# Last block of an attention plus SwiGLU kernel: products P5 and P3 in two PSUM banks, P3 one token tile at a time, the first two token tiles stored in three pieces

## The chip, the cores and the metric

The kernel runs on one core of one Trainium2 chip. The metric is the device time of one execution in microseconds (us), so less is better. A profile of one execution is at hand: every instruction of every engine with its start and duration, and every DMA packet.

## The reference

Attention without a softmax, normalised per head, feeds a gated feed-forward block. Everything is float32.

```python
kv = np.einsum('bhsd,bhse->bhde', k, v)
out = np.einsum('bhsd,bhde->bhse', q, kv)
rms = np.sqrt(np.mean(out * out, axis=-1, keepdims=True) + 1e-06)
x = out / rms * g_norm          # (8, 8, 576, 64), brought to (4608, 512)
g = x @ w_gate                  # (512, 1536)
silu = g * (1.0 / (1.0 + np.exp(-g)))
val = x @ w_val                 # (512, 1536)
result = silu * val @ w_out     # (1536, 512) -> (4608, 512)
```

## The kernel before, in words

The 4608 tokens are cut into nine blocks of 512 (`BLK`), a block into four token tiles of 128. For each block the kernel makes x (attention, transposed), then the hidden values h (the "up" products with w_gate and w_val, silu and multiplication), then the output ("down", the product with w_out). Most large products are done in a Strassen-Winograd form: seven products P1 to P7 of half-size matrices stand in for eight, with sums and differences made by VectorE (DVE) and GpSimd (POOL). From block 2 on the up part applies the form twice, and its prepared weights are streamed from DRAM by the SP queue (line 655).

The class `Down` makes the output of a block. `Ffn.down` (line 835) runs its products in the order 1, 5, 6, 7, 2, 4, 3. `CHAIN` (line 401) says which of three PSUM accumulators a product goes to: 1, 6, 7 and 4 to "b", 2 to "a", 5 and then 3, on top of it, to "c". An accumulator is one PSUM tile of 128 partitions x 2 x 256 float32: two token tiles e = 0 and e = 1, each with 256 output columns. The pool of "c" has two buffers, "b" three, "a" one. `Quad.multiply` (line 420) issues the matmuls of one product: for each e and each of six steps i over the hidden dimension one 128x256 matmul, which the profile shows as two PE matmuls. `Down.order` (line 744) sorts them by i, so e = 0 and e = 1 take turns and both token tiles are complete only with the last matmul.

When a product is complete its `after` function takes the accumulator out:

- after P7 (line 770): ScalarE (ACT) copies "b", DVE adds "c" (P5 alone so far) to it and writes `o2[:, :, HD:DM]`, the right 256 columns of token tiles 2 and 3
- after P2 (line 764): DVE adds "a" and the saved P1 and writes `o1[:, :, 0:HD]`, the left columns of token tiles 0 and 1; then it makes one more difference of h, which P3 reads
- after P4 (line 777): ACT copies "b" to the left columns of `o2`, and `Ffn.store` (line 791) sends `o2` to the output
- after P3 (line 781): DVE adds "c" and the saved P6 (`u2`), writes the right columns of `o1`, and `store` sends `o1`

A store is one DMA on the SP queue, 128 partitions x 2 token tiles x 512 columns, which is listed as 512 KB. Each engine and the SP queue take their instructions in the order in which the program was written; a framework adds the semaphore waits, tile by tile. In the last block (n = 8) nothing follows: after P3 there are one DVE addition, one store and the end of the program.

Of the kernel before, what the change touches and what calls it, by code (L numbers as in the profile page):

```python
# [8 lines left out]
F32 = mybir.dt.float32  # L9
# [5 lines left out]
P = 128  # L15
# [3 lines left out]
def kernel(  # L19
# [41 lines left out]
    nc = tc.nc  # L61

    B, H, S, D = q.shape
    NT, DM = out.shape
    FF = moe_w_gate.shape[1]
    T = 4
    BLK = P * T
    HB = BLK // 2
    HD = DM // 2
    NB = NT // BLK  # L70
# [39 lines left out]
    add = lambda e, o, a, b: e.tensor_tensor(out=o, in0=a, in1=b, op=OP.add)  # L110
# [3 lines left out]
    def ring():  # L114

        return r_pool.tile([P, 4, BLK], F32, name="r")

    class Words:
# [12 lines left out]
        def __init__(self, src, shape):  # L131
            self.raw = ld_pool.tile([P, 2 * BLK], U32, name="ld")
            dst = self.raw.rearrange("p (a b) -> p a b", a=shape[0])
            nc.sync.dma_start(out=dst, in_=src)
            self.shape = shape
# [267 lines left out]
    PSUMS = {"a": a_psum, "b": b_psum, "c": c_psum}  # L403
# [6 lines left out]
    class Quad:  # L410


        def __init__(self, steps):
            self.steps = steps
            self.ps, self.room = {}, None

        def prepare(self):
            pass

        def multiply(self, p):  # L420
            name, first = CHAIN[p]
            if first:
                self.ps[name] = PSUMS[name].tile([P, 2, HB], F32, name=name)
            for e, i in self.order(p):
                lhsT, rhs = self.operands(p, e, i)

                nc.tensor.matmul(  # L427
                    self.ps[name][:, e], lhsT=lhsT, rhs=rhs, start=first and (e, i) == (0, 0),
                    stop=i == self.steps - 1, skip_group_check=True,
                )  # L430
            getattr(self, f"after{p}", lambda: None)()

        def order(self, p):
            return [(e, i) for e in range(2) for i in range(self.steps)]
# [14 lines left out]
    class Up(Quad):  # L449
# [22 lines left out]
        def after2(self):  # L472
            add(nc.vector, self.s, self.ps["a"], self.s)
            nc.scalar.activation(out=self.s, in_=self.s, func=ACT.Silu)

        def after7(self):
            self.u3 = self.piece(2)
            nc.scalar.copy(out=self.u3, in_=self.ps["b"])
            add(nc.vector, self.u3, self.ps["c"], self.u3)
# [6 lines left out]
        def after3(self):  # L486
            add(nc.vector, self.u2, self.ps["c"], self.u2)
            mul(nc.gpsimd, self.h[:, :, 0:HB], self.s, self.u2)
            self.ffn.ended = self.ffn.h_sums(self.j, 1, nc.vector)
# [225 lines left out]
    class Down(Quad):  # L715
        def __init__(self, ffn):
            super().__init__(NP)
            self.ffn = ffn
            self.t = {}

        def turn_t(self, p, after=None):

            pairs = wo.rearrange("p (j e) d -> p e j d", e=2)
            of = {5: pairs[:, 1, :, HD:DM], 7: pairs[:, 0, :, 0:HD], 4: pairs[:, 1, :, 0:HD]}[p]
            self.t[p] = []
            for i in range(0, NP, 2):
                t = t_tile((self.ffn.n, p))
                turned = sub(nc.gpsimd, t, of[:, i : i + 2], pairs[:, 0, i : i + 2, HD:DM])
                if after:
                    tc.add_manual_dep(  # L730
                        turned.ins, after.ins.name,
                        mybir.DependencyInfo(mybir.DependencyClass.Sync, mybir.DependencyReason.DATA), reason="order",
                    )
                self.t[p] += [t[:, 0], t[:, 1]]
# [8 lines left out]

        def order(self, p):
            order = [(e, i) for e in range(2) for i in range(self.steps)]
            return sorted(order, key=lambda ei: ei[1])

        def operands(self, p, e, i):
            h = self.ffn.h
# [13 lines left out]

        def after2(self):
            add(nc.vector, self.o1[:, :, 0:HD], self.ps["a"], self.s)

            pairs = self.ffn.h.rearrange("p (j e) t -> p e j t", e=2)
            sub(nc.vector, pairs[:, 1, :, 0:HB], pairs[:, 1, :, 0:HB], pairs[:, 0, :, HB:BLK])

        def after7(self):  # L770
            o = ring()
            self.o1, self.o2 = o[:, 0:2], o[:, 2:4]
            u3 = self.piece(2)
            nc.scalar.copy(out=u3, in_=self.ps["b"])
            add(nc.vector, self.o2[:, :, HD:DM], self.ps["c"], u3)

        def after4(self):
            nc.scalar.copy(out=self.o2[:, :, 0:HD], in_=self.ps["b"])
            self.ffn.store(self.o2, 2)

        def after3(self):
            add(nc.vector, self.o1[:, :, HD:DM], self.ps["c"], self.u2)
            self.ffn.store(self.o1, 0)

    class Ffn:
        def __init__(self, n, att):
# [1 line left out]
            self.h = h_pool.tile([P, NF, BLK], F32, name="h")  # L788
            self.ps, self.making, self.leaf_room, self.ended = {}, [], None, None

        def store(self, o, t):
            rows = out[BLK * self.n : BLK * (self.n + 1), :].rearrange("(t p) d -> p t d", t=T)
            nc.sync.dma_start(out=rows[:, t : t + 2, :], in_=o)

        def h_sums(self, j, k, engine):

# [105 lines left out]
    for n in range(NB):  # L902
        ffn = Ffn(n, blocks[n])
# [76 lines left out]
```

## Time and profile before

| | |
|---|---|
| time, median of 4 runs | 1067.55 us (1066.72 to 1067.89) |
| the profiled execution's own time | 1066.43 us |
| its span, first to last instruction | 1064.5 us |
| around the span | 1.93 us |
| PE matmul busy | 1039.0 us, 98% of the span |
| DVE, POOL, ACT busy | 66%, 34%, 23% of the span |
| last matmul of P3 ends | 1059.82 us |
| last DVE addition | 1059.85 us, 0.69 us long |
| last store issued on SP | 1060.57 us |

The span runs from the first to the last instruction of the core; what the device time has beyond it lies before or after. A matmul's end in the trace is modelled; the chain of waits counts a product up to where the next work could start. PE is TensorE, SPq the queue from which SP issues DMAs. The time of a DMA in the rows of DMA issues runs from its issue to the landing of its last byte.

### The profile page before, as it was taken

What the parts mean: (1) busy time and instruction counts of PE and PEld (TensorE: products, weight loads), DVE (VectorE), ACT (ScalarE), POOL (GpSimd) and SP (SyncE); (2) the same over time, 40 slices, a digit from 0 to 9 for tenths busy, and PEclk for the clock granted to TensorE, in tenths of its full rate; (3) what the DMA queues carried; (4) which work ended last, traced back from release to release, by engine and by line L of the source; (5) the groups of instructions that cost most, each with busy time, mean ns of one, the idle gap of its engine ahead of it and who ended that gap; (6) DMA issues with size and microseconds to landing.
All of it is one profiled execution on the core that took longest, in us unless ns stands there. A gap on an engine that the chain in (4) does not pass through costs nothing.

```text
span 1064.5 us, 21799 instructions
## 1 busy us (share of the span) xinstructions
PE 1039.0 (98%) x8780; PEld 937.2 (88%) x8780; DVE 701.1 (66%) x1243; ACT 244.9 (23%) x392; POOL 365.5 (34%) x280
## 2 busy tenths in 40 slices
PE   5899999998999999999999999999999999999998
PEld 4644788877899989998999899989999899989997
DVE  2999596768656765676656666666667566755661
ACT  2665111211211211222112212121112211212110
POOL 0000453343025701472156305630455036602670
PEclk9899999999999999999999999999999999999999
DMA  9797103565578326742576247724782366126611
GB/s 242 223 267 226 57 20 101 158 175 162 172 207 243 103 78 190 236 141 61 173 237 174 77 134 231 213 56 131 226 226 70 97 197 192 47 80 203 188 31 40
DMA packets 154356, 161.87 MB, mean 152 GB/s; under 512 B 48400, under 2 KB 105104, under 8 KB 154256
## 3 DMA queue, kind: packets, MB, share of 16 engines
q1 hardware_dynamic: 154192, 160.48, 51.2%
q8 instruction: 70, 1.15, 0.4%
q14 instruction: 30, 0.25, 0.1%
q0 software_dynamic: 64, 0.00, 0.0%
HBM read 138.02 MB, written 22.41 MB: 151 GB/s over the span
## 4 chain that ended last, share of the span: by engine, by line
PE 90%; DVE 4%; SPq 2%; DMA 2%; POOL 1%; issue 1%; ACT 0%; POOLq 0%; DVEq 0%
PE b L576 25%; PE b L427 18%; PE c L576 12%; PE c L427 9%; PE a L576 6%; PE a L427 5%; PE b L861 4%; PE c L861 4%; PE m L339 2%; PE m L255 1%; PE m L292 1%; SPq L223 1%; DVE r L111 1%; DVE xi L111 1%; DVE r L110 1%; PE b L292 1%
## 5 line engine op out<-in xcount | busy, mean ns | idle before, releaser
L110 POOL TENSOR_TENSOR r<-r 128x256 f32<-128x256 f32 (+1 forms) x105 | 110.1, 1054 | 362.9 <-DVE r L110 357.6
L110 DVE TENSOR_TENSOR r<-b,r 128x512 f32<-128x512 f32 (+1 forms) x273 | 162.3, 607 | 61.3 <-PE b L576 56.5
L110 DVE TENSOR_TENSOR r<-c,r 128x512 f32<-128x512 f32 (+1 forms) x177 | 109.0, 626 | 99.3 <-PE c L576 56.0
L111 POOL TENSOR_TENSOR t<-wo 128x512 f32<-128x512 f32 x81 | 112.6, 1415 | 163.9 <-DVE wo L110 107.9
L576 PE MATMUL b<-x,t 128*128 128x128 f32 x1092 | 151.3, 276 | 0.0
L576 PEld LDWEIGHTS b<-x,t 128*128 128x128 f32 x1092 | 136.0, 192 | 0.6
L110 DVE TENSOR_TENSOR r<-a,r 128x512 f32<-128x512 f32 (+1 forms) x99 | 62.6, 633 | 83.2 <-PE a L576 53.1
L112 POOL TENSOR_TENSOR h<-r 128x1024 f32<-128x1024 f32 (+1 forms) x40 | 81.4, 2049 | 93.0 <-DVE r L110 79.7
L576 PE MATMUL c<-xi,t 128*128 128x128 f32 x840 | 112.1, 275 | 0.0
L576 PEld LDWEIGHTS c<-xi,t 128*128 128x128 f32 x840 | 102.8, 192 | 0.0
L427 PE MATMUL b<-t,h 128*128 128x256 f32 x432 | 97.1, 382 | 0.0
L427 PE MATMUL b<-wo,h 128*128 128x256 f32 x432 | 96.2, 379 | 0.0
L427 PEld LDWEIGHTS b<-wo,h 128*128 128x128 f32 x432 | 81.5, 190 | 10.6
L427 PEld LDWEIGHTS b<-t,h 128*128 128x128 f32 x432 | 80.8, 190 | 10.9 <-issue 0.2
L590 ACT COPY r<-b 128x512 f32<-128x512 f32 x63 | 36.9, 585 | 219.1 <-PE b L576 191.8
L576 PE MATMUL b<-xi,t 128*128 128x128 f32 x588 | 79.8, 276 | 0.0
L576 PEld LDWEIGHTS b<-xi,t 128*128 128x128 f32 x588 | 72.4, 192 | 0.0
L576 PE MATMUL b<-x,wg 128*128 128x128 f32 x336 | 53.0, 280 | 0.0
L576 PE MATMUL b<-x,wv 128*128 128x128 f32 x336 | 51.3, 275 | 0.0
L427 PE MATMUL c<-t,s 128*128 128x256 f32 x216 | 48.9, 383 | 0.0
L427 PE MATMUL a<-wo,h 128*128 128x256 f32 x216 | 48.3, 379 | 0.0
L427 PE MATMUL c<-wo,h 128*128 128x256 f32 x216 | 48.1, 379 | 0.0
(129 smaller groups left out, 1650.6 us busy)
## 6 DMA issues: line engine op xcount, KB each, us to landing
t<-w SPq DMA_DIRECT2D x336, 256.0 KB, 3.0
out_dram<-r SPq DMA_DIRECT2D x18, 512.0 KB, 2.9
ld<-in_q_dram SPq DMA_DIRECT2D x29, 256.0 KB, 4.5
ld<-in_moe_w_gate_dram SPq DMA_DIRECT2D x12, 512.0 KB, 5.3
ld<-in_moe_w_val_dram SPq DMA_DIRECT2D x12, 512.0 KB, 5.1
ld<-in_moe_w_out_dram SPq DMA_DIRECT2D x12, 512.0 KB, 4.4
w<-t SPq DMA_DIRECT2D x36, 128.0 KB, 2.1
ld<-in_k_dram SPq DMA_DIRECT2D x26, 160.0 KB, 3.4
```

The source lines that it names most:

```text
L110: add = lambda e, o, a, b: e.tensor_tensor(out=o, in0=a, in1=b, op=OP.add)
L111: sub = lambda e, o, a, b: e.tensor_tensor(out=o, in0=a, in1=b, op=OP.subtract)
L112: mul = lambda e, o, a, b: e.tensor_tensor(out=o, in0=a, in1=b, op=OP.mult)
L223: nc.sync.dma_start(out=t[r * D : (r + 1) * D, :, 0 : m * D], in_=src[self.n, hs, s0 : s0 + m * D].rearrange("h (p t) d -> p h (t d)", t=m),)
L255: nc.tensor.matmul(self.kv_ps[r][u * D : (u + 1) * D, j, :], lhsT=self.k[j][rows, u, c, :], rhs=self.v[j][rows, u, c, :], start=(c == 0), ...
L292: nc.tensor.matmul(self.ps[i][u][p : p + D, t, j, :], lhsT=self.qt[rows, 2 * i + t, j, p : p + D], rhs=kvs[b % 3][rows, j, :], start=True, ...
L339: nc.tensor.transpose(ps[:, e, t], xt[:, t, j + e], ident)
L427: nc.tensor.matmul(self.ps[name][:, e], lhsT=lhsT, rhs=rhs, start=first and (e, i) == (0, 0), stop=i == self.steps - 1, skip_group_check=True,
L576: nc.tensor.matmul(ps[:, i, f], lhsT=self.weight(o, p, f), rhs=self.operand(o, p), start=first and (i, f) == (0, 0), stop=True, skip_group ...
L590: nc.scalar.copy(out=dst, in_=ps)
L861: nc.tensor.matmul(t, lhsT=w[f // 2][:, i, P * (f % 2) : P * (f % 2 + 1)], rhs=x[:, i, of], start=(i == 0), stop=(i == NS - 1),)
```

## The change

Only the last block is touched. There, P5 and P3 get two "c" tiles, one per token tile, instead of one (`apart`); each of the two has its own bank, and only half of each is used. P3 runs all six steps for e = 0 and then all six for e = 1; P5 keeps the alternating order. Both DVE additions that read "c" are split in two, one per token tile (`add_c`). The left columns of `o1` are stored right after P2, and the right columns one token tile at a time after P3, so that `o1` goes out in three DMAs; `o2` is stored as before, now between the first and the second of them.

```diff
@@ class Quad @@
+            self.apart = {}
+
         def multiply(self, p):
             name, first = CHAIN[p]
             if first:
-                self.ps[name] = PSUMS[name].tile([P, 2, HB], F32, name=name)
+                tiles = [PSUMS[name].tile([P, 2, HB], F32, name=name) for _ in range(1 + (name in self.apart))]
+                self.ps[name], self.apart[name] = tiles[0], tiles[-1]
+            banks = self.ps[name], self.apart[name]
             for e, i in self.order(p):
                 lhsT, rhs = self.operands(p, e, i)
 
                 nc.tensor.matmul(
-                    self.ps[name][:, e], lhsT=lhsT, rhs=rhs, start=first and (e, i) == (0, 0),
+                    banks[e][:, e], lhsT=lhsT, rhs=rhs, start=first and i == 0 and (e == 0 or banks[0] is not banks[1]),
                     stop=i == self.steps - 1, skip_group_check=True,
                 )
@@ class Down @@
+            self.final = ffn.n == NB - 1
+            if self.final:
+                self.apart["c"] = None
...
         def order(self, p):
             order = [(e, i) for e in range(2) for i in range(self.steps)]
-            return sorted(order, key=lambda ei: ei[1])
+            return order if p == 3 and self.final else sorted(order, key=lambda ei: ei[1])
...
         def after2(self):
             add(nc.vector, self.o1[:, :, 0:HD], self.ps["a"], self.s)
+            if self.final:
+                self.ffn.store(self.o1[:, :, 0:HD], 0, slice(0, HD))
...
-            add(nc.vector, self.o2[:, :, HD:DM], self.ps["c"], u3)
+            self.add_c(self.o2[:, :, HD:DM], u3)
...
         def after3(self):
-            add(nc.vector, self.o1[:, :, HD:DM], self.ps["c"], self.u2)
-            self.ffn.store(self.o1, 0)
+            self.add_c(self.o1[:, :, HD:DM], self.u2)
+            if not self.final:
+                self.ffn.store(self.o1, 0)
+                return
+            for e in range(2):
+                self.ffn.store(self.o1[:, e : e + 1, HD:DM], e, slice(HD, DM))
+
+        def add_c(self, o, u):
+
+            if not self.final:
+                add(nc.vector, o, self.ps["c"], u)
+                return
+            for e, c in enumerate((self.ps["c"], self.apart["c"])):
+                add(nc.vector, o[:, e], c[:, e], u[:, e])
@@ class Ffn @@
-        def store(self, o, t):
-            rows = out[BLK * self.n : BLK * (self.n + 1), :].rearrange("(t p) d -> p t d", t=T)
-            nc.sync.dma_start(out=rows[:, t : t + 2, :], in_=o)
+        def store(self, o, t, columns=slice(None)):
+            rows = out[BLK * self.n : BLK * (self.n + 1), columns].rearrange("(t p) d -> p t d", t=T)
+            nc.sync.dma_start(out=rows[:, t : t + o.shape[1], :], in_=o)
```

## The prediction

> **What bounds the kernel now.** I read the page first, then the chain of waits of the last 35 us, then the timeline there, then the rows that price the pieces. The page:
>
> ```profile
> span 1064.5 us, 21799 instructions
> ...
> PE 1039.0 (98%) x8780; PEld 937.2 (88%) x8780; DVE 701.1 (66%) x1243; ACT 244.9 (23%) x392; POOL 365.5 (34%) x280
> ...
> PE 90%; DVE 4%; SPq 2%; DMA 2%; POOL 1%; issue 1%; ACT 0%; POOLq 0%; DVEq 0%
> ```
>
> TensorE is the bound, at 98% of the span and 90% of the chain that ended last. The change leaves the number of matmuls as it is, so it can only win where TensorE is already done. The instruction orders of the two programs, which carry no times, are the same on every engine up to P5 of the last block. So everything is decided after about 1028 us. The end of the chain of waits, in order of time (start, length, what):
>
> ```profile
> 1049.45 5.18 PE b L427 x24
> 1054.63 5.19 PE c L427 x24
> 1059.82 0.02 issue
> 1059.85 0.69 DVE r L110
> ```
>
> P4 and P3 run without a gap, 24 PE matmuls in 5.18 and 5.19 us, 0.216 us each. P3 ends at 1059.82, and until the span's end at 1064.5 TensorE does nothing: 4.68 us, in which every step waits for the one before. These are its steps, from the timeline (start, length, engine):
>
> ```profile
> 1045.79 0.69 DVE L110 TENSOR_TENSOR r<-c,r 128x512 f32<-128x512 f32 x1 [14.62 <-ACT r L774]
> ...
> 1049.49 0.69 DVE L110 TENSOR_TENSOR r<-a,r 128x512 f32<-128x512 f32 x1 [3.01 <-PE a L427]
> 1050.10 1.75 DVE L111 TENSOR_TENSOR h<-h 128x1536 f32<-128x1536 f32 x1
> ...
> 1054.74 0.58 ACT L778 COPY r<-b 128x512 f32<-128x512 f32 x1 [8.99 <-PE b L427]
> 1055.36 5.60 SPq L793 DMA_DIRECT2D out_dram<-r  x2
> 1059.85 0.69 DVE L110 TENSOR_TENSOR r<-c,r 128x512 f32<-128x512 f32 x1 [8.00 <-PE c L427]
> ```
>
> The two stores are merged in one line, the second issued at 1060.57. In the DMA view of 1054 to 1064.5 us each slice is 0.26 us:
>
> ```profile
> GB/s 0 0 0 0 0 0 0 0 140 390 382 382 382 312 8 0 0 0 0 0 0 0 0 0 0 0 0 0 179 390 382 390 414 242 0 0 0 0 0 0
> ...
> out_dram<-r SPq DMA_DIRECT2D x2, 512.0 KB, 2.8
> ```
>
> The last store lands 2.8 us after its issue, at 1063.37. Its bytes move from about 1061.48 to 1062.83, 1.35 us at about 390 GB/s. The other 1.45 us (0.9 before the first byte, 0.55 after the last) do not depend on the size in this trace. The tail is then 0.03 + 0.69 (DVE) + 0.03 + 2.8 (store) + 1.13 (closing of the program) = 4.68 us.
>
> **The change, part by part.** The rows for smaller pieces, from the groups kept apart by shape and from the DMA issues:
>
> ```profile
> L110 DVE TENSOR_TENSOR r<-c,r 128x512 f32<-128x512 f32 x135 | 93.3, 691 | 99.3 <-PE c L576 56.0 <-PE c L427 24.1 <-ACT r L774 17.2
> ...
> L110 DVE TENSOR_TENSOR r<-c,r 128x256 f32<-128x256 f32 x42 | 17.4, 415 | 0.0
> ```
>
> ```profile
> w<-t SPq DMA_DIRECT2D x36, 128.0 KB, 2.1
> ...
> w<-r SPq DMA_DIRECT2D x42, 64.0 KB, 1.8
> ```
>
> *The last addition* now covers one token tile: 0.415 us in place of 0.691, **0.28 us** off the path. The addition for e = 0 starts when half of P3 is done, at 1054.63 + 2.59 = 1057.22, ends at 1057.64, and is long out of the way.
>
> *The last store* carries 128 x 256 float32, 128 KB in place of 512. From below: the same 1.45 us fixed and a quarter of 1.35 us, 1.79 us. From above: the stores of prepared weights to DRAM of the same 128 KB take 2.1 us, but in runs of 512 bytes, where the new piece has runs of 1 KB and the old store 2 KB, and with an issue of 0.52 us against 0.39 here. I take 1.9, nearer to the store that this piece is cut from. That is **0.9 us** off the path, 0.7 to 1.0 by the bounds.
>
> *The other pieces.* The left half of `o1` (256 KB) is ready at 1050.18 and has over 5 us before `o2` is issued at 1055.36. Its place on SP is ahead of `o2`, and it waits for the addition after P2, which is done 5 us before `o2`'s own ACT copy; nothing else is on SP behind it, for the last weight load was issued by about 1014.7. The e = 0 piece is issued at about 1057.67. The first store's bytes (`o2`) end at about 1057.7 in the row above, and the e = 0 bytes move around 1058.6 to 1059.0, before the last issue at 1060.29. With that cover gone (two pieces at once) the last one would wait for 0.34 us of bytes.
>
> *One rule against it.* The Trainium skill, "DMA: Bandwidth & Descriptors", section "Anatomy of one DMA", gives a DMA (from the other issuing path, GpSimd's) about 2.0 us fixed plus bytes at 436 GB/s, and its "Rules for kernel authors" says to coalesce many small transfers. If the two added fixed parts were exposed, the split would cost 4.0 us against a gain of about 1.2: 1070.4. The row says otherwise: the fixed part is 1.45 us, and the earlier pieces start 10.1 and 2.6 us before the last, under P4 and P3, so they overlap matmuls. For the last piece alone the formula also gives 0.9 us less (393,216 bytes at 436 GB/s). I follow the row.
>
> *The split addition after P7* costs 2 x 0.415 - 0.691 = 0.14 us. DVE is next needed at 1049.45, by P2's end; it would be done at 1046.62, so this is free. Uncovered it would be 0.14.
>
> *P3 by token tile.* Every matmul loads its own 128x128 weights in either order (24 loads for 24 matmuls). The up part of block 1 runs the e-after-e order already:
>
> ```profile
> 173.88 1.89 PE L427 MATMUL b<-x,t 128*128 128x256 f32 x8
> 175.61 1.89 PE L427 MATMUL c<-x,wv 128*128 128x256 f32 x8
> ```
>
> Eight matmuls from one start to the next are 1.73 us, again 0.216 each: cost 0. DVE reading one bank while TensorE writes another is there now too: at 1049.49 it reads "a" under P4, which keeps its 5.18 us.
>
> *The second bank for P5.* The other "c" buffer is last read by a DVE addition that starts at 1022.44 and ends at 1023.13; P5 starts at about 1028.5, so the wait that its second matmul gets is over 5 us old. Queued behind it would be all of P5; the wait's own handling I bound by 0 and 0.05 us and take 0. P3's first matmul waits for DVE as before: the difference of h started at 1050.10 is done by 1051.85.
>
> *The sum.* 0.28 + 0.9 = 1.18 us off a span of 1064.5, to 1063.3. The profiled execution took 1066.43, 1.93 around the span and 1.1 under the median of the runs; nothing that the change touches lies there. I take 1.18 off the median: 1066.4. About 0.2% (2.1 us) is what a measurement of this kernel can tell from no change, so this is inside it.
>
> **The rivals.**
>
> *Smaller gain: a short store is no quicker.* If the landing is mostly a confirmation that the size doesn't change, only 0.28 us of DVE and perhaps 0.2 remain: 1067.1. For it: 64 KB stores still take 1.8 us, and from 64 to 128 KB the rows gain little. Against: 2.8 for the large one, with 1.35 us of visible bytes.
>
> *The split doesn't take.* If the e = 0 addition waited for all of P3, both additions (0.83) and both stores would follow it: the last issue at about 1060.7, one more quarter of bytes ahead: 1.9 + 0.1. The gain is some 0.6 us: 1066.9. Against: the two tiles are separate, so the waits can be too.
>
> *A gain beyond 0.2%.* It would need 2.1 of the 4.68 us of tail. With the 64 KB row's 1.6 minimum as landing the gain is 1.5: 1066.05. More than that needs the closing 1.13 us to shrink, or the medians to differ by chance; the four runs spread over 1.2 us.
>
> *Slower: TensorE's rate in P5 and P3.* Taking turns between two banks (P5), or staying on one token tile (P3), could open a gap per matmul. There are 48. The gain is used up at 1.18 / 48 = 25 ns each, and the time is over 0.2% longer from (1.18 + 2.13) / 48 = 69 ns each. If the weight loads of P3 (190 ns each) came uncovered, 24 x 0.19 = 4.6 us less 1.18: 1070.9. Against: 0.216 us in both orders above.
>
> **How the numbers follow.** Likeliest case, 1066.4, chance 0.61, its own range 1065.6 to 1067.0 (landing between 1.6 and 2.1, and the medians' scatter). Smaller gain 0.16; the split doesn't take 0.07; beyond 0.2% 0.12; slower 0.04. Faster is the fourth of these, 0.12; slower 0.04; the rest, 0.84, is within 0.2%. The range for 8 in 10 reaches from 1065.3, the edge of the larger gain, to 1067.6, which takes in the smaller ones.
>
> **What would show it.** In the changed kernel's profile: P3 still 5.19 us for 24 matmuls; the next to last DVE addition in the middle of P3 and the last of 0.41 us right after it; the left half's store issued near 1050.2; the last issue 0.44 us after P3's end; its landing 1.8 to 2.1 us later, with bytes for about 0.35 us; 1.1 us from there to the end; a tail of 3.5 us. The prediction is wrong if P5 or P3 lasts longer than 5.3 us, if the last landing stays near 2.8, or if anything ahead of P5 differs.

## The result

| | before | after |
|---|---|---|
| time, median | 1067.14 us (58 runs, 1064.79 to 1068.32) | 1065.55 us (40 runs, 1063.57 to 1066.78) |
| ratio to before | | 0.9986, 95% interval 0.9981 to 0.9990 |
| profiled execution: time, span | 1066.43, 1064.5 us | 1065.77, 1063.9 us |
| from P3's end to the span's end (the tail) | 4.67 us | 3.15 us |
| time around the span, mean | 1.98, 2.01, 2.03 us (49, 29, 33 runs beside the experiments) | 1.82 us (40 runs) |

More runs of the kernel before stand behind this median than behind the one of the prediction, 1067.55. The change makes the kernel 0.14% faster (0.10 to 0.19), 1.5 us of 1067.14 (1.1 to 2.0), within the 0.2% that the prediction called no change. It had said 1066.4, in a range from 1065.3 to 1067.6.

The pages give the span to 0.1 us. Where its end, a landing or a tail stands with two decimals below, it was taken from the time stamps of the same traces, which are in ns: the spans end at 1064.49 and 1063.92. So the old tail is 4.67, where the prediction had 4.68.

### The profile page after: what moved, and what is told of

The parts are those of the page before. It is cut to its first block, busy times and chain, and to the rows that moved or that the text cites. A ratio compares the mean times of both kernels' runs of the same rounds, so it can differ in the third digit from the quotient of the medians.

```text
span 1063.9 us, 21805 instructions
## 1 busy us (share of the span) xinstructions
PE 1038.4 (98%) x8780; PEld 936.1 (88%) x8780; DVE 700.5 (66%) x1245; ACT 245.1 (23%) x392; POOL 366.8 (34%) x280
## 4 chain that ended last, share of the span: by engine, by line
PE 92%; DVE 3%; SPq 2%; DMA 1%; POOL 1%; issue 0%; ACT 0%; DVEq 0%; POOLq 0%
PE b L580 25%; PE b L431 20%; PE c L580 12%; PE c L431 10%; PE a L580 6%; PE a L431 5%; PE c L882 4%; PE b L882 4%; PE m L255 2%; PE m L339 1%; PE m L292 1%; SPq L223 1%; PE b L292 1%; PE b L272 1%; DMA ld<-in_moe_w_gate_dram 1%; PE m L272 1%
```

## The profile after

The page of the changed kernel (`kernel.py` is longer, so line 427 is now 431, and 793 is 814):

```profile
span 1063.9 us, 21805 instructions
...
PE 1038.4 (98%) x8780; PEld 936.1 (88%) x8780; DVE 700.5 (66%) x1245; ACT 245.1 (23%) x392; POOL 366.8 (34%) x280
```

TensorE issues the same 8780 matmuls. Two of the six more instructions are on DVE. The end of the chain of waits (start, length, what):

```profile
1050.40 5.18 PE b L431 x24
1055.58 5.20 PE c L431 x24
1060.77 0.02 issue
1060.80 0.42 DVE r L110
```

P3 takes 5.20 us (5.19 before) and ends at 1060.77; 1063.92 - 1060.77 is the tail of 3.15 us. The timeline of the last block (start, length, engine):

```profile
1046.74 0.76 DVE L110 TENSOR_TENSOR r<-c,r 128x256 f32<-128x256 f32 x2 [14.62 <-ACT r L783]
...
1051.16 10.44 SPq L814 DMA_DIRECT2D out_dram<-r  x4
...
1058.21 0.42 DVE L110 TENSOR_TENSOR r<-c,r 128x256 f32<-128x256 f32 x1 [5.41 <-PE c L431]
1060.80 0.42 DVE L110 TENSOR_TENSOR r<-c,r 128x256 f32<-128x256 f32 x1 [2.16 <-PE c L431]
```

The left half is issued at 1051.16, right after P2's addition (1050.44 to 1051.13). The first right-hand addition stands in the middle of P3, at 1058.21. The DMA view of 1054 to 1063.9 us (slices of 0.25 us), and the issues of 1049 to 1064 us:

```profile
GB/s 0 0 0 0 0 0 0 0 0 0 0 0 17 356 381 389 389 389 199 0 0 0 232 290 8 0 0 0 0 0 0 0 70 356 104 0 0 0 0 0
```

```profile
out_dram<-r SPq DMA_DIRECT2D x1, 512.0 KB, 2.8
out_dram<-r SPq DMA_DIRECT2D x1, 256.0 KB, 2.1
out_dram<-r SPq DMA_DIRECT2D x2, 128.0 KB, 1.7
```

Three separate groups of bytes: `o2`, the piece of token tile 0, the piece of token tile 1. The last piece is issued at 1061.25 and lands 1.71 us later. In finer slices (0.065 us each, from 1060.9 us on) its bytes take eight of them, the first and the last in part:

```profile
GB/s 0 0 0 0 0 0 0 0 0 0 0 0 0 0 0 0 0 0 110 347 315 378 347 315 174 32 0 0 0 0 0 0 0 0 0 0 0 0 0 0
```

From the start of its first DMA packet to the end of its last one it is 0.52 us, and 1.51 us for the old last store, which landed 2.84 us after its issue, at 1063.40.

**Why the spans differ by 0.6 us and the tails by 1.52.** P3 ends 0.95 us later in this execution than in the profiled one of before. The two programs are the same up to P5, and TensorE works without a gap and does the same 6509 matmuls from 300 to 1000 us in both (columns: stretch, its length, PE busy and its count, PE weight loads, DVE, ACT, POOL, clock, DMA share, GB/s). Before:

```profile
300.00:1000.00 700.00, 700.00 (x6509) 667.38 (x6508) 450.83 (x759) 140.90 (x216) 272.63 (x206) 1.00 0.52 155
```

After:

```profile
300.00:1000.00 700.00, 700.00 (x6509) 667.10 (x6509) 450.15 (x758) 141.59 (x217) 271.75 (x206) 1.00 0.52 155
```

So the 0.95 us arose before 300 us, where TensorE has idle time in both. Over the ten profiled executions of this study P5 starts anywhere from 1028.51 to 1030.27. From here on, tails are compared, counted from P3's end in the chain of waits.

**A part outside the span.** The time around the span (a run's time less its span) is shorter too: on average 1.82 us in the 40 runs of the changed kernel, and 1.98, 2.01 and 2.03 in three sets of runs of the kernel before. Runs of both kernels taken side by side on one chip have 1.82 and 2.03. It is 0.16 to 0.21 us that neither the prediction nor the theory below has. It goes with the way of storing: 2.00 with banks and split additions but one whole store, 1.87 with the left half stored early, 1.76 and 1.77 with the last piece halved. What happens in this time stands in no trace, so the cause stays open. With it the traces give 1.7 us in all, within the 1.1 to 2.0 of the runs.

## The experiments

The theory that the experiments test: the gain of the span lies in the tail alone, and is the sum of a shorter last addition, a shorter last store, and a shorter closing of the program. "Closing" is what comes after the landing of the last store.

### The early store of the left half alone

```diff
 after2:
             add(nc.vector, self.o1[:, :, 0:HD], self.ps["a"], self.s)
+            if self.ffn.n == NB - 1:
+                self.ffn.store(self.o1[:, :, 0:HD], 0, slice(0, HD))
 after3:
-            self.ffn.store(self.o1, 0)
+            if self.ffn.n == NB - 1:
+                self.ffn.store(self.o1[:, :, HD:DM], 0, slice(HD, DM))
+            else:
+                self.ffn.store(self.o1, 0)
 (store takes columns, as in the change)
```

> Only the early store of the left columns is kept: one bank, P3 alternating, one last addition, and one last store of 256 KB. The tail is counted from the end of P3 in the chain of waits to the span's end (4.68 us before, 3.13 after the whole change). Theory (the gain is made of a shorter last addition, a shorter last store and a shorter closing): addition 0.69, store about 2.1, closing about 1.04, tail 3.9, time about 0.8 us under the kernel before. Rival (the size of the last store does not matter): tail 4.7. Rival (the early store alone is the whole gain): tail 3.1.

Measured: the ratio to before is 0.9993 (0.9985 to 1.0001), which alone doesn't tell it from no gain. The chain's end and the issues of the last 15 us:

```profile
1055.43 5.19 PE c L427 x24
1060.62 0.02 issue
1060.64 0.69 DVE r L110
```

```profile
out_dram<-r SPq DMA_DIRECT2D x2, 256.0 KB, 2.1
```

The span ends at 1064.54, so the tail is 3.92 us, as the theory had it: half of the tail's gain (0.75 of 1.52) needs neither a second bank nor a new order, only a last store of half the size.

### The banks, the order and the split additions, with one store

```diff
 (from the changed kernel)
 after2:
-            if self.final:
-                self.ffn.store(self.o1[:, :, 0:HD], 0, slice(0, HD))
 after3:
-            if not self.final:
-                self.ffn.store(self.o1, 0)
-                return
-            for e in range(2):
-                self.ffn.store(self.o1[:, e : e + 1, HD:DM], e, slice(HD, DM))
+            self.ffn.store(self.o1, 0)
```

> Two banks, P3 by token tile and the split additions are kept, but o1 is stored whole, 512 KB, at the end. Theory: last addition 0.42, store 2.8, closing 1.13, tail 4.41, time 0.27 us under the kernel before, which the rounds can hardly tell from none. Rival (the banks and the order of P3 themselves make TensorE or the end quicker): tail near 3.1 or P3 shorter than 5.18. Rival (they slow it): P5 or P3 over 5.3 us.

Measured: 1.0003 (0.9995 to 1.0011). In its chain P3 is as long as ever, and the addition is short:

```profile
1056.27 5.19 PE c L431 x24
1061.46 0.02 issue
1061.48 0.42 DVE r L110
```

P5 takes 5.18 us in the same chain. The span ends at 1065.86: a tail of 4.40 us, where 4.41 was expected. The second bank and the order cost TensorE nothing and bring nothing but the 0.27 us of the addition, which the runs' interval doesn't show.

### P3 alternating, the rest of the change kept

```diff
-            return order if p == 3 and self.final else sorted(order, key=lambda ei: ei[1])
+            return sorted(order, key=lambda ei: ei[1])
```

> The whole change but for the order of P3, which alternates between the token tiles as before, so that both additions and both right-hand stores follow P3's end. Theory: the last store is issued 0.90 us after P3's end in place of 0.48, lands 1.7 to 1.8 later, tail 3.55. Rival (the order of P3 is worth nothing): tail 3.13. Rival (the two last stores hold each other up): landing over 2.1, tail over 3.9.

Measured: 0.9989 (0.9983 to 0.9996), and a tail of 3.21 us. The expectation of 3.55 was wrong, and the chain shows why:

```profile
1055.47 4.76 PE c L431 x22
1060.23 0.02 issue
1060.26 0.42 DVE r L110
1060.68 0.01 issue
1060.69 0.42 DVE r L110
```

The first addition follows after 22 of 24 PE matmuls. With a bank for each token tile, tile 0 is complete one 128x256 matmul (two PE matmuls, 0.43 us) before tile 1, and the addition takes 0.42. So it is done when P3 ends, at about 1055.47 + 5.19 = 1060.66, and the second starts 0.03 us later, as in the changed kernel. Its store is issued at 1061.15, 0.49 us after P3's end; I had expected both additions behind P3. With two banks, the order of P3 is worth 0.06 us, 0.05 of it in the landing (1.76 us after the issue, against 1.71).

### The left half stored last

```diff
 after2:
-            if self.final:
-                self.ffn.store(self.o1[:, :, 0:HD], 0, slice(0, HD))
 after3, behind the two right-hand stores:
+            tc.add_manual_dep(
+                self.ffn.store(self.o1[:, :, 0:HD], 0, slice(0, HD)).ins, self.last.ins.name,
+                mybir.DependencyInfo(mybir.DependencyClass.Sync, mybir.DependencyReason.DATA), reason="order",
+            )
 (self.last is the last addition of add_c; store returns its DMA)
```

> The whole change, but the store of the left columns (256 KB) waits for the last addition and is issued last, right behind the last right-hand store. Theory (fixed parts of stores overlap): issued 0.39 us after the other one, landing 2.1 to 2.3, tail 3.9 to 4.1. Rival (each further store at the end pays its fixed part in full, about 1.4 us by the trace or 2.0 by the rule): tail 4.9 to 5.5.

Measured: 0.9994 (0.9986 to 1.0003). The two stores behind P3's end (1059.81) are merged in one line of the timeline; their issues end after 0.81 us:

```profile
1060.28 0.81 SPq L816 DMA_DIRECT2D out_dram<-r  x2
```

```profile
out_dram<-r SPq DMA_DIRECT2D x2, 128.0 KB, 1.7
out_dram<-r SPq DMA_DIRECT2D x1, 256.0 KB, 2.2
```

The span ends at 1063.85: a tail of 4.04 us, within what the theory gave. The exposed store costs 0.89 us more than the hidden one: 0.38 for the issue ahead of it, and 0.51 because 256 KB land later than 128 (2.22 us after the issue, against 1.71). No fixed part is paid twice; a last store of 256 KB alone landed after 2.16 us in the first experiment.

### The last store on another semaphore

The tails held 0.13 us more gain than the addition and the store account for: the closing is 1.09 us before (1063.40 to 1064.49) and 0.96 after (1062.96 to 1063.92). The 1.13 of the prediction came from rounded figures. The traces name the semaphore of each DMA: the DMAs on SP take eight completion semaphores in turn, and at the end SP waits for all of them in six instructions, one after the other, in the same order in every kernel. To shift the last store's semaphore, two stores that are hidden under matmuls were cut by token tile:

```diff
 after2:
-                self.ffn.store(self.o1[:, :, 0:HD], 0, slice(0, HD))
+                for e in range(2):
+                    self.ffn.store(self.o1[:, e : e + 1, 0:HD], e, slice(0, HD))
 after4:
-            self.ffn.store(self.o2, 2)
+            if not self.final:
+                self.ffn.store(self.o2, 2)
+                return
+            for e in range(2):
+                self.ffn.store(self.o2[:, e : e + 1], 2 + e)
```

> The whole change, and the store of the left columns and the store of o2 are each cut in two by token tile, with no work added or left out, so that the last store uses completion semaphore 0 of the eight that the stores take in turn (before: 4, changed kernel: 6). Theory of the closing (SP waits for the eight one after the other, so what is behind the last store's one comes after its landing): closing 1.3 to 1.5 in place of 0.95, tail 3.5 to 3.7. Rival (the closing's 0.18 us between the kernels is scatter or rounding): tail 3.1.

Measured: 0.9984 (0.9978 to 0.9991), P3's end at 1060.14, the span's at 1063.56, so a tail of 3.42 us; issue at 1060.62, landing 1.70 later, and a closing of 1.24. Both are just below what was expected, and well above the 3.15 and 0.96 of the changed kernel. SP's own instructions at the end, from 1060.9 us on (count, shortest/median/longest in ns, first and last start):

```profile
L1001 SPq EVENT_SEMAPHORE  x8: 17/28/1282, 1061.0 to 1063.5; - x8
```

One wait takes 1282 ns, the one for the last store; four of the waits for the other semaphores come behind it. In the two kernels themselves each of the six waits shows its 28 ns once it can start, between 1061.0 and 1063.6 before and between 1061.6 and 1063.0 after. Behind them stands SP's first drain.

The time stamps split the closing in two there. From the landing to the drain, each wait that is left costs 0.06 us:

| kernel | waits left when the last store has landed | landing to drain, us | drain to the span's end, us |
|---|---|---|---|
| before; banks with one store | 4 | 0.27 | 0.82 |
| early store | 3 | 0.21 | 0.82 |
| changed kernel; P3 alternating; left half last | 2 | 0.14 | 0.82 |
| last piece halved | 1 | 0.08 | 0.93 |
| this experiment | the store's own, then 4 | 0.31 | 0.93 |

So the 0.13 us between the two kernels are two waits of 0.06 us, a by-product of issuing two more stores, and with two more again it was lost. But this experiment's longer closing is only in part an effect of the semaphore: 0.17 of the 0.28 us over the changed kernel lie in the waits, and 0.11 behind the drain, where SP's third drain comes late and takes 130 ns, in place of 7. The kernel with the halved piece has the same 0.11. The record doesn't show why. The ratio of the runs resolves none of this.

### The last piece halved

The one version that could beat the changed kernel: the second token tile cut into two halves of 128 columns, the last addition and store 128 x 128.

```diff
 Down.multiply, last block, P5 and P3 in place of the inherited loop:
+                    c0, c1 = (c_psum.tile([P, 2, HB], F32, name="c") for _ in range(2))
+                    self.parts = [(0, 0, HB, c0), (1, 0, P, c1), (1, P, HB, m_psum.tile([P, 2, HB], F32, name="m"))]
+                pairs = [(part, i) for part in self.parts for i in range(self.steps)]
+                for (e, x, y, c), i in pairs if p == 3 else sorted(pairs, key=lambda pi: pi[1]):
+                    lhsT, rhs = self.operands(p, e, i)
+                    nc.tensor.matmul(
+                        c[:, e, x:y], lhsT=lhsT, rhs=rhs[:, x:y], start=p == 5 and i == 0,
+                        stop=i == self.steps - 1, skip_group_check=True,
+                    )
 (add_c and the stores run over self.parts)
```

> The whole change, and the second token tile of P5 and P3 is cut once more, into two halves of 128 columns, each in a bank of its own (the second one taken from the pool m, idle in the last block); the last addition and the last store are 128 x 128. Theory: addition 0.28, store 1.6, closing 0.9, tail 2.85, and P3 still 5.2 us; time 0.3 us under the changed kernel, less than the rounds tell. Rival (matmuls of 128 columns are slowed by their weight loads): P3 over 5.6 us and no gain. Rival (the store is at its floor): landing 1.7, tail 3.0.

Measured: 0.9978 (0.9968 to 0.9988).

```profile
1056.03 3.93 PE c L751 x24
1059.96 1.35 PE m L751 x12
1061.31 0.02 issue
1061.34 0.29 DVE r L110
```

```profile
out_dram<-r SPq DMA_DIRECT2D x1, 64.0 KB, 1.5
```

The span ends at 1064.20: a tail of 2.89, where 2.85 was expected. But P3 takes 3.93 + 1.35 = 5.28 us, 0.08 more, and P5 5.27, 0.09 more. The gain of 0.26 us in the tail is mostly given back: some 0.09 are left. (Its closing has the 0.11 us of the experiment before.) The ratio looked better than that, so both kernels were run once more side by side.

> The changed kernel once more, beside the halved last piece on one chip. Theory (only the tail differs): tail 3.1 again, wherever P5 starts; ratio to before 0.9985 within 0.0007. Rival (something ahead of P5 differs too): a tail other than 3.1, or a ratio outside that.

> The halved last piece once more. Theory: tail 2.9 and P3 5.28, in all 0.15 to 0.25 us under the changed kernel, which the rounds can't tell from none. Rival (the 0.0008 between the two ratios measured so far is real): 0.8 us or more under the changed kernel in the same call.

Measured: the changed kernel 0.9985 (0.9979 to 0.9992), tail 3.15; the halved piece 0.9991 (0.9983 to 0.9999), tail 2.89, P3 again 5.28. Both tails came out the same to 0.01 us, though P5 started 0.45 us later and 1.43 us earlier than the first time. Side by side the halved piece was behind, not 0.8 us ahead; its two intervals overlap, and its first ratio did not repeat. It is no measurable improvement.

## Why the prediction was right, point by point

| us | before | predicted | measured |
|---|---|---|---|
| last addition | 0.69 | 0.415 | 0.42 |
| last store, issue to landing | 2.84 | 1.9 | 1.71 |
| closing | 1.09 | 1.13 | 0.96 |
| tail, with two handovers of 0.03 | 4.67 | 3.5 | 3.15 |
| gain in the tail | | 1.18 | 1.52 |
| gain around the span | | 0 | 0.16 to 0.21 |
| gain by the runs | | 1.18 | 1.5 (1.1 to 2.0) |

The time itself came out 0.85 us under the 1066.4. About half of that, 0.41, is the starting point: the median of four runs was 1067.55, that of 58 is 1067.14. The rest is the gain, which was taken too small in two of the three steps of the tail and at nothing around the span.

- *What bounds it, and that all is decided behind P5*: right within the span. Both have the same matmuls, P5 and P3 are within 0.02 us of before, and but for the halved piece the variants differ behind P3's end. The scatter ahead of P5, up to 1.76 us from one execution to another, is larger than the gain, which is why only many runs show it.
- *The last addition*: right, 0.42. The chain of the kernel with one store showed it alone.
- *The last store*: right in kind, too long by 0.2. The prediction leant from its lower bound (1.79) towards the row of 128 KB stores in runs of 512 bytes (2.1). Its split of the old store was read from slices: by the packets the bytes run from 1061.47 to 1062.98, 1.51 us and not 1.35, with 0.90 before them and 0.42 after, not 0.55. The new piece takes 0.84, 0.52 and 0.35. So its bytes took more than a quarter (0.38), and the part outside them was not independent of size: 1.19 us, against 1.32. That the lower bound came within 0.08 us is luck: it had 0.18 too little for the bytes and 0.26 too much outside them. Of the 0.13 us, 0.04 are the issue (0.34 us in place of 0.39). The landings of the last stores are 2.84 us for 512 KB, 2.16 for 256, 1.71 for 128 and 1.53 for 64.
- *The closing*: a step that failed in size. The prediction kept it at 1.13 with no reason given; two more stores move the last one on by two semaphores, and SP has two waits fewer behind its landing, 0.13 us.
- *Around the span*: "nothing that the change touches lies there" failed, by 0.16 to 0.21 us, and why is open.
- *The rule against it*: the Trainium skill's formula for GpSimd's path ("DMA: Bandwidth & Descriptors", "Anatomy of one DMA") would make the last piece 2.3 us, an estimate by 2.0 fixed plus 131,072 bytes at 436 GB/s; it took 1.71 on SP's queue. Its advice to coalesce many small transfers ("Rules for kernel authors") did not fit the end of this kernel, where the pieces become ready at different times: the same additions with one whole store had a tail of 4.40 us, with three pieces 3.15. A further store exposed at the very end cost 0.89 us, less than the 1.27 that a last store of 256 KB takes outside its bytes.
- *The other pieces, the split addition after P7*: hidden, as said. The pair takes 0.76 us, 0.07 more than one, not 0.14: by the time stamps the second starts 0.08 us before the first ends. DVE was needed 2.9 us later.
- *The second bank and the order of P3*: free, as said. What the prediction missed is that the order is hardly needed: with two banks the alternating P3 already lets token tile 0 out 0.43 us early, just the length of its addition.
- *The rivals*: the short store that is no quicker fell with 1.71 us; the split that doesn't take fell with the addition at 1058.21; the slower TensorE fell with 5.18 and 5.20 us. Whether one bank would do was not tried: DVE would then read the bank that TensorE is writing, and no run here shows what that costs.

One sentence ahead of the prediction was too simple: the engines do not take their instructions strictly in the order of the text. In the chain of the kernel before, four PE matmuls of P2 (0.86 us from 1038.99) come ahead of P7, which the text puts first.

## What to carry to other kernels

Where the bounding engine has finished, the rest is a chain, and it is priced step by step: only the piece that becomes ready last counts, so store everything else earlier and make that piece small. Half of the tail's gain came from the plainest edit, sending what was ready; look for it before banks and loop orders. A gain smaller than the scatter of whole executions is read from the part of the trace that can differ, and confirmed by many runs.

## What was not expected of the hardware

- A store's time outside its bytes is not quite constant: 1.32 us for 512 KB, 1.27 for 256, 1.19 for 128 and 1.18 for 64, each the last store of its kernel.
- The end of a program depends on which completion semaphore the last store uses, because SP waits for all of them in a fixed order, 0.06 us each: 0.08 to 0.31 us from landing to drain over the ten traces.
- The time around the span depends on how the last block is stored, 1.76 to 2.03 us on average. The cause is open.
- Matmuls of 128 columns in place of 256, for one of P3's two token tiles, cost 0.08 us in some 2.6 (both times that it was profiled).
